# Both products of the MLP by one level of Strassen's algorithm, layer 1 in full before layer 2

## The chip, the cores and the metric

One core of a Trainium2 chip runs the kernel. The metric is the device time of one execution in microseconds. Each time that follows is that of such an execution; a profile is one execution taken by the hardware profiler.

## The reference

2048 tokens of 640 channels go through two sublayers, each with a layer norm, a shift and scale from a condition vector, and a gate. Sublayer A is a causal depthwise convolution along the sequence by way of a Fourier transform; sublayer B is an MLP with squared ReLU. All data are float32.

```
mod = (_silu(c) @ w_mod).reshape(c.shape[0], 6, 1, -1)
sa, ca, ga, sb, cb, gb = ...
h = _layernorm(q, axis=-1) * (1 + ca) + sa
x = q + ga * _A_ref(h, k, v, shift_k, ssm_k, ssm_D)
h = _layernorm(x, axis=-1) * (1 + cb) + sb
h = relu(h @ w1 + b1) ** 2          # w1: 640 x 1728
x = x + gb * (h @ w2 + b2)          # w2: 1728 x 640
```

## The kernel before

The program is recorded as a graph of operations and then ordered by a list scheduler (`Graph.order`, line 227), which runs a model of the five engines and emits each engine's instructions in the order it found. An operation's priority is either a number in the table `URGE` (by group, as ("f1", 0) for layer 1 of chunk 0) or, where the table has none, the longest path from it to the end (`levels`, line 189). After that the order on each engine is fixed, and the engines meet at semaphores. Every recorded operation shows line 444 in the profile, so groups are told apart by their tiles.

**The first part** (to about 277 us of the profile) is sublayer A: for five blocks of 128 channels, transforms by matmuls in plain float32, products of spectra on DVE and POOL, and back. Its result x1 goes to DRAM (`x1_d`), but for the first 512 tokens, which stay in SBUF. Weights of the MLP are loaded and split in its last 50 us.

**The MLP** multiplies by a split: each operand is written as a high part (rounded to fp32r by ACT) and a low part (the rest, by DVE or POOL), and a product is three matmuls: high x high, high x low, low x high. The tokens go in 8 chunks of 256 (`NC`), the inner dimension of 1728 in 14 blocks of 128 (`NF`; the last has 64). For each chunk: `prep_hat` and `prep_xt` (lines 1204, 1213) normalise, transpose, scale and split the tokens into the tile `xt`; for each block f, `mlp_front` (1231) makes layer 1 into one PSUM bank from five k-blocks, `mlp_middle` (1250) adds the bias, squares and splits h into a ring of six small tiles (`hring` and others), and `mlp_back` (1275) multiplies h with w2 into four accumulators of 320 columns; `mlp_out` (1299) multiplies by the gate row, adds x1 and stores. From chunk 1 on, layer 1 takes high x (high, low) in one matmul of 512 columns and low x high in one of 256. All of w1 and w2 stays in SBUF, split (`w_load`, 1146, into tiles `w_S...`, `w_W...`, `w_KA...`). The gate row is made by ten float32 matmuls on a broadcast condition (`w_gate`, lines 1677 to 1697) around the end of the first part, and b2 times the gate is added to x1 by POOL.

The chunks overlap freely: layer 1 of a later block or chunk runs between layer 2 of an earlier one.

Of the kernel before, what the change touches and what calls it, by code (L numbers as in the profile page):

```python
# [29 lines left out]
LAST = 690.0  # L30
# [85 lines left out]
class Buf:  # L116
    __slots__ = ("name", "shape", "dtype", "choices", "real", "cell", "seen", "users", "n", "line", "psum", "left", "end")
# [6 lines left out]
class Graph:  # L124
    def __init__(self):
        self.nodes, self.group, self.bufs = [], None, []
        self.key, self.urge = ("", 0), {}

    def buf(self, name, shape, dtype, choices, cell=32, line=None, psum=False):
# [6 lines left out]
        b.line, b.psum, b.real, b.seen, b.users, b.n = line, psum, None, [], set(), len(self.bufs)  # L136
        self.bufs.append(b)
# [51 lines left out]
    def levels(self):  # L189
# [6 lines left out]
        for b in self.bufs:  # L196
            if len(b.choices) == 1:
                for s in b.choices[0][0]:
                    if s in line:
                        later.setdefault(line[s].n, []).append(b)  # L200
                    line[s] = b
        level = [0.0] * len(nodes)
        blevel = {}
        for n in reversed(nodes):
# [22 lines left out]
    def order(self, lag=0.06, pelag=0.1, phase=0.0):  # L227
# [82 lines left out]
        def early(n):  # L310
            return 1e4 if not n.told else HOLD if n.engine == "SP" and n.key[0] != "out" else 30.0 if n.key[0] == "warm" else 1e4
# [198 lines left out]
def ssm_mlp_kernel(  # L510
# [80 lines left out]
    KV = sb.tile([P, 5120], F32, tag="KV", name="KV")  # L591
    WX = sb.tile([P, 5120], F32, tag="WX", name="wx")
# [17 lines left out]
    work = [part(lambda: WX, 512 * i, (f"W{i}",)) for i in range(10)]  # L610
    work += [part(lambda: WE, 512 * i, (f"W{10 + i}",)) for i in range(2)]
    KACC = [part(lambda: KV, 512 * i, (f"KA{i}",)) for i in range(2)]
    KN = [part(lambda: KV, 1024 + 1024 * i, (f"KN{i}a", f"KN{i}b")) for i in range(4)]
    UT = [part(lambda: KV, 3072 + 512 * i, (f"KN{2 + i // 2}{'ab'[i % 2]}",)) for i in range(4)]
    KVALL = (("KA0", "KA1") + tuple(f"KN{i}{h}" for i in range(4) for h in "ab"), lambda s, d, n: sb.tile(s, d, tag="KV", name=n))
# [12 lines left out]
    def sbuf(name, shape, choices, dtype=F32, line=None):  # L628
        return g.buf(name, list(shape), dtype, choices, line=line)
# [487 lines left out]
    def x1_tile(n):  # L1117
        return sbuf(f"x1_{n}", (P, 2, D), [whole("X1a"), whole("X1b")], line="X1")
# [668 lines left out]
```

## Time and profile before

| | |
|---|---|
| median of 3 runs | 678.6 us (677.04 to 680.27) |
| span of the profiled execution | 678.1 us (the page gives no time around it) |
| TensorE matmul busy | 659.3 us |
| VectorE, ScalarE, GpSimd busy | 408.6, 317.2, 257.2 us |
| first MLP product | 277.29 us |
| HBM read, written | 56.98 MB, 14.42 MB |

PE is TensorE's matmuls, PEld its weight loads, DVE is VectorE, ACT ScalarE, POOL GpSimd, SP the engine that issues most DMAs. A row of a timeline has start, length, engine, operation, "out<-in" by the program's tile names, and a count where like instructions follow each other. A row of a group has, behind the bar, busy time and the mean of one in ns, and then the idle time of its engine before it with what ended it. Matmuls overlap in the pipeline, so the length of one (some 300 ns) is not what it adds to the time; the distance between starts is.

### The profile page before, as it was taken

What the parts mean: (1) busy time and instruction counts of PE and PEld (TensorE: products, weight loads), DVE (VectorE), ACT (ScalarE), POOL (GpSimd) and SP (SyncE); (2) the same over time, 40 slices, a digit from 0 to 9 for tenths busy, and PEclk for the clock granted to TensorE, in tenths of its full rate; (3) what the DMA queues carried; (4) which work ended last, traced back from release to release, by engine and by line L of the source; (5) the groups of instructions that cost most, each with busy time, mean ns of one, the idle gap of its engine ahead of it and who ended that gap; (6) DMA issues with size and microseconds to landing.
All of it is one profiled execution on the core that took longest, in us unless ns stands there. A gap on an engine that the chain in (4) does not pass through costs nothing.

```text
span 678.1 us, 16426 instructions
## 1 busy us (share of the span) xinstructions
PE 659.3 (97%) x6825; PEld 597.1 (88%) x6825; DVE 408.6 (60%) x813; ACT 317.2 (47%) x650; POOL 257.2 (38%) x330
## 2 busy tenths in 40 slices
PE   9989999999899999999999999999999999999996
PEld 8879698789788796899999999999989999999996
DVE  2759677988689767766436562554563562663532
ACT  3654858887655846555225242243232242242220
POOL 2439467779767684362014031021031040040001
PEclk9999999999899999999999999999999999999999
DMA  9799999997785473433020200110110100200011
GB/s 226 222 269 299 265 251 200 260 259 203 186 201 116 90 229 125 126 94 92 1 78 1 78 1 1 22 58 1 23 55 1 44 36 1 69 10 1 4 37 39
DMA packets 108430, 72.45 MB, mean 107 GB/s; under 512 B 48514, under 2 KB 95810, under 8 KB 108356
## 3 DMA queue, kind: packets, MB, share of 16 engines
q1 hardware_dynamic: 106304, 70.80, 40.2%
q8 instruction: 53, 0.87, 0.6%
q10 hardware_dynamic: 1988, 0.61, 0.4%
q14 instruction: 21, 0.17, 0.1%
q0 software_dynamic: 64, 0.01, 0.0%
HBM read 56.98 MB, written 14.42 MB: 105 GB/s over the span
## 4 chain that ended last, share of the span: by engine, by line
PE 83%; DVE 6%; DMA 3%; ACT 3%; issue 2%; POOL 1%; ACTq 0%; SPq 0%; DVEq 0%; POOLq 0%
PE ps L444 83%; DVE KV L444 2%; DMA KV<-in_A_v_dram 1%; DVE mtmp L444 1%; DMA x<-x_d 1%; POOL wx L444 1%; DMA d<-in_A_ssm_D_dram 1%; ACT q L444 1%; DVE s L444 1%; DVE wx L444 1%; DMA out_dram<-x 1%; ACT up L444 1%; POOL wm L444 0%; ACT KV L444 0%; ACT a L444 0%
## 5 line engine op out<-in xcount | busy, mean ns | idle before, releaser
L444 PE MATMUL ps<-xt,w_S 128*128 128x512 f32 (+1 forms) x935 | 174.7, 329 | 0.0
L444 PEld LDWEIGHTS ps<-xt,w_S 128*128 128x128 f32 x935 | 140.9, 188 | 13.5 <-DVE w_S L444 0.2
L444 PE MATMUL ps<-w_S,hring 128*128 128x320 f32 x648 | 110.5, 311 | 0.0
L444 ACT ACTIVATE mtmp<-ps,b1t 128x256 f32<-128x256 f32 (+1 forms) x112 | 50.2, 474 | 112.2 <-PE ps L444 107.2
L444 PEld LDWEIGHTS ps<-w_S,hring 128*128 128x128 f32 x648 | 99.2, 188 | 2.2
L444 DVE TENSOR_TENSOR mtmp<-ps,mtmp 128x256 f32<-128x256 f32 (+1 forms) x99 | 40.5, 419 | 74.2 <-ACT mtmp L444 73.8
L444 PE MATMUL ps<-a,gb 128*64 128x128 f32 x1260 | 76.1, 275 | 3.8 <-DVE wx L444 2.1
L444 PEld LDWEIGHTS ps<-a,gb 128*64 128x64 f32 x1260 | 69.3, 137 | 10.7 <-DVE wx L444 3.3
L444 DVE TENSOR_TENSOR hring<-mtmp,hring 128x256 fp32r<-128x256 f32 x74 | 38.6, 525 | 49.3 <-ACT hring L444 48.8
L444 PEld LDWEIGHTS ps<-cst,p 64*64 64x64 f32 (+1 forms) x1792 | 58.4, 135 | 10.9 <-issue 6.8
L444 PE MATMUL ps<-cst,p 64*64 64x64 f32 (+1 forms) x1792 | 63.9, 244 | 2.4 <-issue 2.2
L444 POOL TENSOR_TENSOR wx<-wx 128x256 f32<-128x256 f32 x80 | 59.8, 766 | 10.6 <-DVE wx L444 8.5
L444 ACT ACTIVATE hring<-mtmp 128x256 fp32r<-128x256 f32 x74 | 30.9, 418 | 69.4 <-PE ps L444 50.5
L444 POOL TENSOR_TENSOR x<-x,gb2row 128x640 f32<-128x640 f32 x16 | 25.6, 1618 | 88.5 <-ACT mtmp L444 73.6
L444 ACT ACTIVATE a<-ps 128x512 f32<-128x512 f32 x72 | 41.3, 616 | 34.2 <-PE ps L444 33.8
L444 POOL TENSOR_TENSOR x<-mtmp,x 128x640 f32<-128x640 f32 (+1 forms) x9 | 13.3, 1483 | 115.5 <-DVE mtmp L444 115.5
L444 PE MATMUL ps<-w_S,w_W 128*128 128x320 f32 x312 | 53.5, 311 | 0.3 <-DVE w_W L444 0.3
L444 PEld LDWEIGHTS ps<-w_S,w_W 128*128 128x128 f32 x312 | 47.7, 188 | 1.4 <-DVE w_W L444 0.6
L444 DVE TENSOR_TENSOR wx<-ps,wx 128x512 f32<-128x512 f32 x64 | 40.7, 681 | 13.0 <-PE ps L444 7.8
L444 DVE SCALAR_TENSOR_TENSOR mtmp<-mtmp 128x256 f32<-128x256 f32 x91 | 43.7, 493 | 1.7
L444 POOL TENSOR_TENSOR mtmp<-mtmp 128x256 f32<-128x256 f32 (+1 forms) x21 | 13.4, 645 | 82.5 <-ACT mtmp L444 82.5
L444 PE MATMUL ps<-gi,wx 64*128 64x128 f32 x640 | 41.8, 284 | 0.0
(142 smaller groups left out, 1092.8 us busy)
## 6 DMA issues: line engine op xcount, KB each, us to landing
wm<-in_w_mod_dram SPq DMA_DIRECT2D x25, 320.0 KB, 4.8
p<-in_A_ssm_k_dram SPq DMA_DIRECT2D x20, 256.0 KB, 4.9
KV<-in_A_k_dram SPq DMA_DIRECT2D x20, 256.0 KB, 4.2
KV<-in_A_v_dram SPq DMA_DIRECT2D x20, 256.0 KB, 5.0
p<-kv_d SPq DMA_DIRECT2D x20, 256.0 KB, 4.6
xp<-in_A_q_dram SPq DMA_DIRECT2D x10, 512.0 KB, 7.8
q<-in_A_q_dram SPq DMA_DIRECT2D x7, 640.0 KB, 5.2
out_dram<-x SPq DMA_DIRECT2D x14, 320.0 KB, 3.8
```

Of the source, the lines that this page charges most:

```text
L444: fn(*real, **{k: a.real() if isinstance(a, View) else a for k, a in kw.items()})
```

## The change

Two matrices cut into 2 x 2 blocks are multiplied with 7 block products in place of 8 (Strassen's scheme in Winograd's form: sums of blocks on both sides, and intermediate sums of products that are used twice). Here this is one level, over the split products as before.

**Layer 1** goes over 4 quarters s of 512 tokens (two chunks a and b) and 6 pairs p of f-blocks. Four of the five k-blocks form the 2 x 2 cut; the fifth is added plainly. A pair takes 18 block products of 128 x 128 x 256 in place of 20. Three PSUM banks x, z, y per pair (two sets in turn) accumulate; x is read by ACT in the middle of its accumulation and then goes on. The last two f-blocks are done plainly (`rest`). The squared result, not split, is stored to a new tensor in DRAM, `h_d`.

**Layer 2** goes over 8 chunks of 256 tokens (two halves i) and the 6 pairs of f-blocks, with seven accumulators of 320 columns (`ps7`), in place of four; block products per pair: 7 for 8. h is read back from DRAM by pairs (two pairs in one tile from chunk 1 on), four sums are made on DVE, and the seven pieces of 128 are split (ACT, DVE) into a ring of four (`ring2`). At the end of a chunk one copy and seven additions join the accumulators. b2 rides as a row in the last w2 block, times a block of ones.

The weights are split with their sums: `w1_pair` on POOL and DVE before and during the first quarter, `w2_pair` in the tiles of w1 as the last quarter frees them. The gate row becomes one sum on POOL and two matmuls, in the first quarter. The large tiles KV and WX are cut in two each.

In the scheduler the numbers of all MLP groups are gone from `URGE`; they are placed by the longest path, with each TensorE operation of the MLP charged its place in the program's order (`turns`), and an early limit for SP and other engines.

```diff
-LAST = 690.0
+LAST = 640.0
+AHEAD = 60.0
+SPARE = 10.0
+LAG = 0.1
...
+            top += LAG
+            if n.engine == "PE" and n.id >= self.mlp:
+                turns = top = max(top, turns)
+                turns += n.cost
...
+    def w1_pair(p):
+        split(w[:, 0, 0:5], w[:, 1, 0:5], r1)
+        split(w[:, 0, 5:8], w[:, 1, 5:8], r2[:, 2:5])
+        for j, (eng, op, l, r) in enumerate((
+            (pool, add, r2[:, 0:2], r2[:, 2:4]),
+            (pool, sub, 0, r1[:, 0:2]),
+            (dve, sub, r1[:, 0:2], r2[:, 0:2]),
+            (pool, sub, r1[:, 2:4], 1),
+            (pool, sub, r1[:, 4:5], r2[:, 4:5]),
+        )):
...
+    def combined(s):
+        halves(2 * s + 1, T2)
+        for j, (l, r) in enumerate(((c[:, 0:2], a[:, 0:2]), (c[:, 2:4], 0), (c[:, 2:4], c[:, 0:2]), (a[:, 2:4], 1))):
+            sub(dve, t, l, made[r] if isinstance(r, int) else r)
+            split(TC[j][:, 0], TC[j][:, 1], t)
...
+    def pair(s, p, before):
+        products(x, [(wb(i), xa(i)) for i in range(2)], True, True)
+        taken(r1[:, 0:CH], x, c1)
+        before()
+        products(z, [(wb(i + 2), xa(i + 2)) for i in range(2)] + [(wb(4), xa(4))], True, True)
+        plus(r1[:, 0:CH], z)
+        products(y, [(wb(8 + i), tc_(0, i)) for i in range(2)] + [(wb(7), xb(4))], True, True)
+        taken(r2[:, CH:], y, c2)
+        products(x, [(wb(10 + i), tc_(1, i)) for i in range(2)], False, True)
+        taken(r1[:, CH:], x, c1)
+        products(y, [(wb(14 + i), xb(i + 2)) for i in range(2)] + [(wb(16), xb(4))], False, True)
+        plus(r1[:, CH:], y)
+        square(r1)
+        h_store(s, f1, r1)
+        products(x, [(wb(12 + i), tc_(2, i)) for i in range(2)], False, True)
+        plus(r2[:, CH:], x)
+        def after():
+            products(x, [(wb(5 + i), tc_(3, i)) for i in range(2)] + [(wb(7), xa(4))], False, True)
+            taken(r2[:, 0:CH], x, c2)
+            square(r2)
+            h_store(s, f2, r2)
...
+    def h_pair(n, p, many=1):
+            sp_dma(t[:, k, 0:4].rearrange("p (j i) t -> p j (i t)", j=2), in_dram(h_d, src, f, f + 2 * P, 1 << n // 2), 1024)
+        add(dve, t[:, :, 4], t[:, :, 0], t[:, :, 2])
+        sub(dve, t[:, :, 5], t[:, :, 4], t[:, :, 1])
+        sub(dve, t[:, :, 6], t[:, :, 1], t[:, :, 0])
+        sub(dve, t[:, :, 7], t[:, :, 3], t[:, :, 5])
+        for k in range(many):
+            h = HS[n, p + k] = ring2[(n * NP + p + k) % 4]
+            split(h[:, 0], h[:, 1], t[:, k, 1:8])
...
+    def l2(acc, h, w, first, last):
+        with g.as_one(0.441):
+            for i, (a, y) in enumerate(((0, 0), (0, 1), (1, 0))):
+                mm(acc, h[a], w[y], first and i == 0, last and i == 2)
+    def second_layer(n):
+        todo = {1: (0, 0), 2: (2, 1), 6: (4, 4), 7: (5, 5), 4: (1, 6), 5: (3, 3), 3: (6, 2)}
+            for i, (a, b) in todo.items():
+                l2(ps7[i], parts(h, a), wv, p == 0, p == NP - 1)
+        copy(act, e1, ps7[1])
+        add(dve, c[:, 1, 0], ps7[2], e1)
+        add(dve, u2, ps7[6], e1)
+        add(dve, u3, ps7[7], u2)
+        add(dve, c[:, 0, 0], ps7[4], u3)
+        add(dve, u2, ps7[5], u2)
+        add(dve, c[:, 0, 1], ps7[5], u3)
+        add(dve, c[:, 1, 1], ps7[3], u2)
```

Where the first part ends, TensorE's order before (`mtmp` are the normalised tokens, `xt` the split ones, `w_S` weights, `wx`/`we` and `cst` the last transforms of the first part):

```order
L444 MATMUL ps_94<-ident,mtmp 128x128
L444 MATMUL ps_93<-ident,mtmp 128x128
L444 MATMUL ps_98<-w_gate 128x320
L444 MATMUL ps_97<-we,cst 64x512
L444 MATMUL ps_97<-wx,cst 64x512
L444 MATMUL ps_98<-w_gate 128x320 x3
L444 MATMUL ps_95<-xt_3701,w_S_2622 128x256 x6
L444 MATMUL ps_97<-xt_3701,w_S_2622 128x256 x3
L444 MATMUL ps_98<-xt_3701,w_S_3407 128x256 x6
```

and after (`up` holds the normalised tokens, `t_0` the split first chunk, `ka` the first two sums of token blocks, `xa` the second chunk, `w_0` and `w_1` the first two weight pairs):

```order
L458 MATMUL ps_99<-we,cst 64x512
L458 MATMUL ps_99<-wxb,cst 64x512
L458 MATMUL ps_93<-ident,up_1718 128x128 x2
L458 MATMUL ps_94<-ident,up_1718 128x128 x2
L458 MATMUL ps_98<-ident,up_1718 128x128 x2
L458 MATMUL ps_95<-t_0_3763,w_0_3025 128x256 x3
L458 MATMUL ps_96<-t_0_3763,w_1_3317 128x256 x3
L458 MATMUL ps_95<-t_0_3763,w_0_3025 128x256 x3
L458 MATMUL ps_94<-t_0_3763,w_0_3025 128x256 x3
L458 MATMUL ps_96<-t_0_3763,w_1_3317 128x256 x3
```

The gate's products are gone from there, the transposes of two chunks stand before the first product in place of one chunk's, and the first products of two pairs alternate.

On DVE at the same place, before (`xfs` are scaled transposes, `xt` their low halves):

```order
L444 TENSOR_TENSOR w_S_3617<-w1s_3587,w_S_3617 128x640
L444 TENSOR_SCALAR xfs<-ps_91,cbs 128x256
L444 TENSOR_TENSOR up_1007<-ps_97,up_1007 128x512
L444 TENSOR_TENSOR xt_3701<-xfs,xt_3701 128x256 x2
L444 TENSOR_TENSOR gb2row<-ps_98,gb2row 128x320
L444 BN_AGGR mv_3636<-s_2495 128x2
L444 TENSOR_SCALAR xfs<-ps_93,cbs 128x256
L444 TENSOR_TENSOR xt_3701<-xfs,xt_3701 128x256
```

and after (`s` holds the last two weight blocks, `we<-xf` are the sums of token blocks):

```order
L458 TENSOR_TENSOR w_4_3715<-up_1718,w_4_3715 128x256
L458 TENSOR_TENSOR s_3643<-w1s_3503,s_3643 128x5x64
L458 TENSOR_SCALAR xf<-ps_93,cbs 128x256
L458 TENSOR_SCALAR xf<-ps_98,cbs 128x256
L458 TENSOR_SCALAR xf<-ps_95,cbs 128x256
L458 TENSOR_TENSOR t_0_3763<-xf,t_0_3763 128x256
L458 TENSOR_TENSOR we<-xf 128x512
L458 TENSOR_TENSOR t_0_3763<-xf,t_0_3763 128x256
L458 TENSOR_SCALAR xf<-ps_97,cbs 128x256
L458 TENSOR_TENSOR t_0_3763<-xf,t_0_3763 128x256
L458 TENSOR_SCALAR xf<-ps_93,cbs 128x256
L458 TENSOR_TENSOR t_0_3763<-xf,t_0_3763 128x256
```

More of the weights' splits are ahead of the first token block, and sums of 512 columns stand between the token blocks' low halves.

In layer 2, around the end of a chunk, DVE's order after the change (`outs` is the joining of the accumulators, `up` the h read back with its sums, `ka`, `kz`, `xa`, `xp1r` the four places of the split ring):

```order
L458 TENSOR_TENSOR up_1718<-up_1718 128x2x128
L458 TENSOR_TENSOR outs<-ps_94,outs 128x320
L458 TENSOR_TENSOR outs<-ps_95,outs 128x320
L458 TENSOR_TENSOR kz<-up_1010,kz 128x896
L458 TENSOR_TENSOR outs<-ps_96,outs 128x320
L458 TENSOR_TENSOR outs<-ps_97,outs 128x320
L458 TENSOR_TENSOR xa<-up_1010,xa 128x896
L458 TENSOR_TENSOR outs<-ps_100,outs 128x320 x2
L458 TENSOR_TENSOR up_1718<-up_1718 128x2x128 x3
L458 TENSOR_TENSOR outs<-ps_99,outs 128x320
L458 TENSOR_TENSOR outs<-outs,gbrow 128x640
L458 TENSOR_TENSOR xp1r<-up_1718,xp1r 128x896
```

Splits of the next chunk's h stand between the additions that free the accumulators; before, DVE's work there was one split of 256 per f-block and four multiplications by the gate per chunk.

More of the change, by code (lines that the diff above doesn't have):

```diff
@@ new lines, in ssm_mlp_kernel, with first_layer @@
+    late = [lambda: None]
+    def first_layer(s):
+        for p in range(NP):
+            late[0] = pair(s, p, late[0])
+            if p == 3 and s + 1 < NS:
+                tokens(s + 1)
+            if s == NS - 1 and p == 4:
+                ring_two()
+                h_pair(0, 0)
+        r = [out_tile(f, s) for f in (NF - 2, NF - 1)]
+        rest(s, 1, r)
+        if s == NS - 1:
+            h_pair(0, 1)
+        late[0]()
+        late[0] = lambda: None
+        if s + 1 < NS:
+            combined(s + 1)
+        rest(s, 0, r)
+        g.key = ("ev", s)
+        square(r[0])
+        square(r[1][:64])
+        h_store(s, NF - 2, r[0])
+        h_store(s, NF - 1, r[1], 64)
```

612 lines of the change are left out of this document (360 added, 252 removed), and 77 rows, old and new, of the table URGE.

## Prediction

> **What bounds the kernel now.** I read the page's head and first part, then the busy time by stage, then who made TensorE wait, then TensorE's timeline where products of one width follow each other.
>
> ```profile
> span 678.1 us, 16426 instructions
> PE 659.3 (97%) x6825; PEld 597.1 (88%) x6825; DVE 408.6 (60%) x813; ACT 317.2 (47%) x650; POOL 257.2 (38%) x330
> ...
> 277.00:323.00 46.00, 45.97 (x347) 45.01 (x346) 28.86 (x47) 25.85 (x55) 19.82 (x22) 1.00 0.37 103
> 358.00:481.00 123.00, 122.66 (x790) 115.17 (x789) 61.97 (x146) 42.82 (x97) 26.18 (x26) 1.00 0.08 22
> 504.67:668.00 163.33, 163.33 (x1049) 154.01 (x1050) 76.01 (x179) 50.18 (x117) 27.66 (x27) 1.00 0.08 21
> ...
> PE ps L444 <- ACT mtmp L444: 0.3, 1, 0.3
> PE ps L444 <- DVE w_W L444: 0.3, 1, 0.3
> ```
>
> In the stage rows the columns are length, then PE, PEld, DVE, ACT and POOL busy, granted clock, DMA share. In 163.33 us of the MLP TensorE has no gap at full clock, DVE is busy 47%, DMA 8%. The only waits of TensorE that fall in the MLP are the last two rows, 0.6 us together. So the MLP lasts as long as its matmuls, and DVE, ACT and the DMAs have room. A change that takes columns from TensorE is paid in full until something else is late.
>
> **TensorE's term.** The price of a product by its width, from starts of neighbouring groups:
>
> ```profile
> 286.32 3.00 PE L444 MATMUL ps<-xt,w_S 128*128 128x256 f32 x24
> 289.16 0.60 PE L444 MATMUL ps<-w_S,w_W 128*128 128x320 f32 x3
> ...
> 435.99 6.48 PE L444 MATMUL ps<-xt,w_S 128*128 128x256 f32 x36
> 442.30 1.92 PE L444 MATMUL ps<-w_S,w_W 128*128 128x320 f32 x12
> ...
> 661.03 3.69 PE L444 MATMUL ps<-w_S,hring 128*128 128x320 f32 x24
> 664.55 0.60 PE L444 MATMUL ps<-w_W 128*128 128x320 f32 x3
> ...
> L444 PE MATMUL ps<-xt,w_S 128*128 128x512 f32 x18 | 6.2, 395 | 0.0
> L444 PE MATMUL ps<-xt,w_S 128*128 128x256 f32 x18 | 4.7, 280 | 0.0
> ```
>
> 24 products of 256 columns took 289.16 - 286.32 = 2.84 us, 0.1183 us each. 24 of 320 took 664.55 - 661.03 = 3.52 us, 0.1467 each. The group at 435.99 is 18 of 512 and 18 of 256 (last two rows); 6.31 us for it leaves 0.232 for one of 512. Before, the code issues in layer 1 455 wide and 730 narrow products (chunk 0: 13 x 15 + 10 narrow; each later chunk 65 wide, 75 narrow) and in layer 2 8 x (13 x 12 + 8) = 1312 of 320: 105.7 + 86.4 + 192.5 = 384.6 us. After, layer 1 has 24 pairs x 18 block products x 3 plus 8 x 25 = 1496 of 256, and layer 2 8 x (6 x 7 x 3 + 20) = 1168 of 320: 177.0 + 171.3 = 348.3 us. **Removed: 36.3 us.** It is not an eighth, as one of five k-blocks in layer 1 and the last two f-blocks stay plain.
>
> The Trainium skill, "TensorE: Matmul & The Clock Gate", section "Back-to-back issue gap", speaks against this term: it gives a sustained 81 ns per matmul at 128 columns and 131 ns at 512, so half the width costs far more than half. Drawn as a line (an estimate from that page) both versions would cost about 270 us and nothing would be removed. By the trace a line through 0.1183 and 0.1467 has under 0.01 us at no columns, so the trace does not agree.
>
> **The start of the MLP.** Before, DVE's last copy of the first part's transform starts at 262.19 and the first product at 277.29:
>
> ```profile
> 262.19 0.68 DVE L444 COPY q<-ps 128x512 f32<-128x512 f32 x1
> ...
> 272.97 1.25 PE L444 MATMUL ps<-ident,mtmp 128*128 128x128 f32 x10
> 274.06 0.70 PE L444 MATMUL ps<-w_gate 128*128 128x320 f32 x2
> ...
> 275.70 1.88 PE L444 MATMUL ps<-w_gate 128*128 128x320 f32 x6
> 277.29 8.32 PE L444 MATMUL ps<-xt,w_S 128*128 128x256 f32 x63
> ...
> L444 PE MATMUL ps<-w_gate 128*128 128x320 f32 x20 | 6.9, 454 | 0.0
> ...
> L444 DVE TENSOR_TENSOR xt<-xfs,xt 128x256 fp32r<-128x256 f32 x5 | 2.0, 423 | 0.3 <-ACT xt L444 0.3
> L444 DVE TENSOR_TENSOR mtmp<-ps,gbrow 128x320 f32<-128x320 f32 x32 | 14.5, 485 | 15.9 <-PE ps L444 15.8
> L444 DVE TENSOR_TENSOR wx<-ps,wx 128x512 f32<-128x512 f32 x64 | 40.7, 681 | 13.0 <-PE ps L444 7.8 <-POOL wx L444 2.7 <-issue 2.5
> L444 DVE TENSOR_TENSOR x<-mtmp,x 128x640 f32<-128x640 f32 x7 | 5.8, 824 | 0.2
> L444 DVE SCALAR_TENSOR_TENSOR mtmp<-mtmp 128x256 f32<-128x256 f32 x91 | 43.7, 493 | 1.7
> ```
>
> The gate's 20 matmul records go (6 in 1.59 us at 275.70, so 5.3 us), and 4 come back later. I count nothing for them: TensorE would only wait longer, since DVE feeds the first product. DVE's price is 0.42 us for 256 columns, 0.48 for 320, 0.68 for 512, 0.82 for 640, by that slope 1.09 for 896; with three operands 0.49 for 256, so 0.76 for 512; in a row each starts 0.07 earlier than that. (Ten transposes, 272.97 to 274.06, are 0.11 each.) From the copy to the low half of the first token block DVE had 28 instructions before (13.0 us); after, 43 (17.9 us: four pairs' weight splits and combinations are finished first). That is 4.8 us more on an engine that idled about 2 us there. Against it TensorE and ACT do less there. I take the first product at 281.3, **4.0 later** (bounds 0, if DVE's idle time and other engines absorb it; 8, if the weight work queued ahead also delays the first part). Then 14 more DVE instructions (the second chunk and the four sums) pace the next 21 block products, 7.4 us on TensorE: 0.8 more (0 to 2).
>
> **The first quarter of layer 1.** TensorE needs 374 x 0.1183 = 44.2 plus 20 transposes and the gate, 47.5 us. DVE's order holds 105 instructions there (37 of 512, 14 of them with three operands, 23.9 us; 48 of 256, 16.7; the rest 6.0), 46.6 us by the prices above. POOL's eight weight differences (5.5 us) and the gate's four sums (6.3) stand beside it. A POOL operation and a DVE operation on SBUF hold each other up:
>
> ```profile
> L444 POOL TENSOR_TENSOR wx<-wx 128x256 f32<-128x256 f32 x80 | 59.8, 766 | 10.6 <-DVE wx L444 8.5 <-DMA xp<-in_A_q_dram 1.4
> L444 POOL TENSOR_TENSOR wm<-wm,wm 128x640 f32<-128x640 f32 x20 | 31.4, 1572 | 15.1 <-ACT wm L444 14.8
> ...
> L444 ACT ACTIVATE mtmp<-ps,b1t 128x256 f32<-128x256 f32 x104 | 46.4, 474 | 105.5 <-PE ps L444 100.6 <-DVE hring L444 3.6 <-DVE w_W L444 1.1
> ...
> 286.06 3.45 POOL L444 TENSOR_TENSOR x<-x,gb2row 128x640 f32<-128x640 f32 x2
> ...
> 286.59 1.51 DVE L444 TENSOR_TENSOR hring<-mtmp,hring 128x256 fp32r<-128x256 f32 x1 [0.20 <-ACT hring L444]
> ```
>
> The DVE operation took 1.51 us instead of 0.42. By these rows POOL pays 0.77 us for 256 columns and 1.57 for 640, ACT 0.47 for an accumulator. If a third of POOL's 12 us falls on DVE, DVE needs 51; TensorE has two pairs of PSUM banks as slack: **2.5 us** (0 to 8). The other quarters have 31 to 33 us of DVE work for 46: 0.5 each, 1.5 (0 to 4). There the new waits (an accumulator may go on only when ACT has read it) have 9 block products or 3.2 us of cover against ACT's 0.47; behind a waiting product every other accumulator's products queue, so a late ACT would show at once. The 56 stores of h (256 KB, some one per 3 us) meet a DMA that is 8% busy; SP's queue holds them in DVE's order, ahead of weights needed 10 us later.
>
> **Between the layers.** Layer 2's weights reuse layer 1's tiles, and h comes back from DRAM. From the last product of layer 1 to the first that needs pair 5 stand some 19 to 21 us of TensorE work; DVE has 23 us listed by then and just after (splits of h, two weight pairs), POOL eight subtractions of about 0.85. I take **3 us** (0 to 8).
>
> **Layer 2.** A chunk of 256 tokens is 146 x 0.1467 = 21.4 us. DVE has per chunk 12 sums of 256 (0.35), 6 splits of 896 (1.02), the last block 1.4, seven additions from PSUM (0.41) and four of 640 (0.75): 17.6 us, 82%, without POOL beside it. All seven accumulators end within 3 us and eight banks exist, so a late DVE operation stops TensorE at the next chunk's first pair. Cover there is 2.6 us per bank, against up to 1.1 us of a split ahead of it. I take 0.5 per chunk, **4 us** (0 to 16). The reads of h must also arrive:
>
> ```profile
> p<-kv_d SPq DMA_DIRECT2D x20, 256.0 KB, 4.6
> ...
> x_d<-xp SPq DMA_DIRECT2D x15, 256.0 KB, 3.4
> x<-x_d SPq DMA_DIRECT2D x6, 640.0 KB, 4.1
> ```
>
> A double pair is 2 x 256 KB, so between 4.1 and 9.2 us. A buffer serves three doubles (load X, then 3.5 us on DVE) and one last block (about 6.4) in two chunks, 42.8 us: 3X + 16.9 fits up to X = 8.6. I take X = 6, hidden; at 9.2 it is 0.9 us a chunk. SP's queue puts a chunk's stores and the residual's load ahead of the next reads; I leave that to the range.
>
> **The end.** After the last product, before:
>
> ```profile
> 671.30 1.19 PE L444 MATMUL ps<-w_KA,hring 128*128 128x320 f32 x7
> 672.53 0.49 DVE L444 TENSOR_TENSOR mtmp<-ps,gbrow 128x320 f32<-128x320 f32 x1 [0.24 <-PE ps L444]
> 672.94 0.89 DVE L444 TENSOR_TENSOR x<-mtmp,x 128x320 f32<-128x320 f32 x2
> ```
>
> TensorE ends at 672.5, DVE at 673.8, the span 4.3 later. After, DVE still owes about two PSUM additions, four multiplications and four additions of 320 (0.41 each), 4.3 us, then the same 4.3: **3.2 us more** (2 to 4.5). Transposes (80 before and after) cancel; the moved gate (five loads of 320 KB on SP between weight loads and x1's stores, five ACT scalings, four POOL additions, two products) is needed only at chunk 0's output, some 190 us later, and hurts only by POOL's share above.
>
> **The sum.** Before, 277.3 + 384.6 + 7.7 of transposes would end at 669.6; it ended at 672.5, so 2.9 us were small losses that my terms replace. 678.1 - 36.3 - 2.9 + 4.0 + 0.8 + 2.5 + 1.5 + 3 + 4 + 3.2 = 657.9; with 10 transposes counted inside the old start, 1.1 less, and the gate back, 1.1 more, it stays. I round to 658. The page gives no time around the span; the median of the runs, 678.6, is 0.5 above it, within their spread of 3.2, so 658 stands for both.
>
> **Rivals.**
> - *TensorE bounds throughout.* The start costs 0 to 1, DVE's lateness is absorbed, only the end is longer: 678.1 - 36.3 - 2.9 + 1 + 3.2 + 1 = 644. For it: DVE is under 85% nearly everywhere and the before stages show no gap. Against: the first quarter's 46.6 of 47.5. Chance 0.22 (640 to 650).
> - *DVE becomes the bound of the first quarter and of layer 2.* All of POOL's 12 us fall on DVE (+8), and each chunk loses 1.5 us: 658 + 5.5 + 8 = 671. Chance 0.15 (665 to 676).
> - *The reads of h pace layer 2, and it is slower.* Place: the two h buffers. 20 us of forecast gain are 2.5 a chunk, 5 in two: 3X + 16.9 = 47.8, X = 10.3. At X = 12, 53 us per two chunks, about 41 more: 699. The longest row is 2 x 4.6; the reads wait behind other transfers on one queue. Chance 0.05. The same side would be reached if a product cost by number and not by columns: the 36.3 go and 694 is left, which the rates above exclude to a hundredth, 0.01.
> - That it doesn't do what it says is excluded: TensorE's order holds exactly 1496 and 1168 products.
>
> **Chances.** Forecast 0.57 (650 to 665), the others as above. The range leaves out about 0.1 at each end: 643 to 673. About 0.5% (3.4 us) is what a measurement of this kernel can tell from no change; faster by more than that 0.92, within it 0.03, slower 0.05.
>
> **What would show it.** Right: 256-wide products still at 0.118 us and 320-wide at 0.147; the first product near 281; DVE near 90% busy for the 48 us after it and waits of TensorE there; layer 2 at 21.5 to 22.5 us a chunk with DVE about 82% busy; 8.5 us from the last product to the end. Wrong: DVE idle while TensorE waits in layer 2 (then the reads of h), a price per product that grew, or a first part that ends later.

## The result, and the profile after

| | before | after |
|---|---|---|
| median | 679.4 us (677.04 to 680.27, 4 runs) | 689.39 us (689.02 to 689.64, 4 runs) |
| span of the profiled execution | 678.1 us | 687.2 us |
| first MLP product | 277.29 us | 301.12 us |

After to before is 1.0155, 95% interval [1.0134, 1.0177]: slower by 1.6%. Forecast were 658 us and a gain of 3%. The profiled execution of the changed kernel took 689.02 us, 1.8 more than its span.

The head of the page of the changed kernel, with the clock's row (40 slices of 17.2 us, tenths of full speed):

```profile
span 687.2 us, 17238 instructions
PE 637.4 (93%) x6976; PEld 589.4 (86%) x6976; DVE 521.9 (76%) x981; ACT 359.1 (52%) x685; POOL 223.7 (33%) x294
PEclk9999999999999999569999999999998999999998
```

TensorE is busy 21.9 us less, and yet the span is 9.1 longer: idle time came in. The dip of the clock, slices 17 and 18, lies where the MLP begins. The busy time by stage of the changed kernel (length; PE, PEld, DVE, ACT, POOL busy with counts; clock; DMA share; GB/s):

```profile
175.00:220.00 45.00, 41.11 (x780) 34.82 (x778) 33.37 (x55) 23.83 (x49) 29.28 (x39) 0.98 0.77 172
220.00:240.00 20.00, 16.39 (x531) 14.41 (x530) 12.67 (x23) 15.81 (x35) 12.81 (x12) 0.91 0.28 55
240.00:271.00 31.00, 29.14 (x497) 24.79 (x488) 26.29 (x41) 17.39 (x37) 24.55 (x32) 1.00 0.24 65
271.00:301.00 30.00, 19.58 (x67) 9.92 (x68) 21.56 (x45) 12.37 (x29) 8.92 (x10) 0.58 0.53 167
301.12:357.25 56.13, 51.50 (x402) 50.21 (x401) 44.25 (x97) 36.57 (x76) 10.32 (x9) 0.95 0.34 108
357.25:497.25 140.00, 139.24 (x1164) 137.86 (x1164) 101.25 (x204) 74.88 (x153) 18.38 (x18) 1.00 0.38 126
497.25:530.00 32.75, 27.51 (x157) 25.15 (x156) 29.00 (x54) 14.74 (x24) 7.23 (x7) 0.90 0.40 120
530.00:676.00 146.00, 146.00 (x997) 146.00 (x997) 120.32 (x222) 46.05 (x66) 0.00 (x0) 1.00 0.44 138
```

and the same view of the kernel before, where the first part ends:

```profile
175.00:220.00 45.00, 43.65 (x874) 37.96 (x872) 37.19 (x62) 27.12 (x55) 30.04 (x40) 0.97 0.72 164
220.00:240.00 20.00, 19.88 (x555) 14.79 (x555) 14.85 (x21) 16.59 (x35) 11.65 (x11) 1.00 0.44 98
240.00:261.00 21.00, 21.00 (x367) 20.05 (x364) 14.82 (x21) 12.26 (x22) 19.01 (x27) 1.00 0.66 203
```

TensorE's busy time is 2.5 us less by 220 and 3.5 less from 220 to 240, in a part whose arithmetic the change doesn't touch; then it is idle for a third of the last 30 us before the MLP. The second to fourth quarter and layer 2 after 530 are full. TensorE's timeline of the changed kernel has the marks between the stages:

```profile
268.18 2.50 PE L458 MATMUL ps<-gi,wxb 64*128 64x128 f32 x32 [0.77 <-ACT q L458]
...
301.12 4.61 PE L458 MATMUL ps<-t,w 128*128 128x256 f32 x27
...
320.75 1.65 PE L458 MATMUL ps<-xa,w 128*128 128x256 f32 x6 [3.91 <-ACT up L458]
...
354.13 3.12 PE L458 MATMUL ps<-t,s 128*128 128x256 f32 x25
...
494.13 3.12 PE L458 MATMUL ps<-t,s 128*128 128x256 f32 x25
497.09 1.92 PE L458 MATMUL ps<-w,xp1r 128*128 128x320 f32 x12
...
677.71 1.04 PE L458 MATMUL ps<-w,xa 128*128 128x320 f32 x6
```

The last groups of 25 end a quarter each (25 x 0.1183 = 3.0 us). In the table each piece stands against the forecast's (137.1 is 1122 products at 0.1183 and 40 transposes at 0.11):

| piece | forecast | measured | over |
|---|---|---|---|
| up to the first MLP product | 281.3 | 301.12 | +19.8 |
| first quarter with its pacing | 47.5 + 0.8 + 2.5 = 50.8 | 354.13 + 3.0 - 301.12 = 56.0 | +5.2 |
| other three quarters | 137.1 + 1.5 = 138.6 | 497.09 - 357.1 = 140.0 | +1.4 |
| change of layers and layer 2 | 171.3 + 3 + 4 = 178.3 | 677.71 + 6 x 0.1467 - 497.09 = 181.5 | +3.2 |
| end | 8.5 | 687.2 - 678.6 = 8.6 | +0.1 |

The forecasts of the pieces add to 657.5, 0.4 us under the sum as it was stated; with the 29.7 over they make 687.2. Two thirds of the miss lie before the first product. The kernel before ended its last inverse transform of that kind at 260.9, of which this row of its timeline has the start:

```profile
255.29 5.63 PE L444 MATMUL ps<-gi,wx 64*128 64x128 f32 x96
```

After, the same group ends at 268.18 + 2.50 = 270.7. So 9.8 us are lost before that mark, and the stretch from it to the first product went from 16.4 to 30.4 us, 14.0 more. The chain that ended last, of the changed kernel, names what the first part of that stretch waits for (start, length, what):

```profile
269.69 0.88 POOL up L458
...
270.63 0.53 POOL up L458
...
271.18 3.40 DMA w1s<-in_B_w_dram
...
274.60 0.74 ACT w L458
...
275.37 0.26 DVE w L458
275.63 0.48 issue
276.11 0.95 DVE up L458
277.06 0.61 DVE we L458
277.68 0.04 issue
277.72 2.00 PE ps L458 x4
```

Read it backwards. TensorE's transforms at 277.72, the first of the first part's last four such groups, wait for DVE's copy `we`, a step of the first part. That copy stands in DVE's queue behind a weight's low half (`w`) and a sum of weights (`up`). The low half waits for ACT's high half, that one for a weight load, and the load for its staging buffer `w1s`, which POOL had held until its last sum of weights was made. The low half is the fourth of six of 640 columns on DVE, one for each weight pair, so it belongs to the fourth pair. In TensorE's order that pair's first product is the 115th of the MLP, and it starts here:

```profile
315.97 0.87 PE L458 MATMUL ps<-t,w 128*128 128x256 f32 x6
```

So the first part waits for weights that TensorE reads 38 us later. Later in the chain the same shows once more: the last group of transforms, at 297.30, waits for a copy that stands behind 2.1 us of weights' low halves on DVE (from 294.51). DVE is 72% busy in the stretch (21.56 of 30 us); no engine is full.

### The profile page after: what moved, and what is told of

It is laid out like the page before. It is cut to its first block, busy times and chain, and to the rows that moved or that the text cites. A ratio compares the mean times of both kernels' runs of the same rounds, so it can differ in the third digit from the quotient of the medians.

```text
span 687.2 us, 17238 instructions
## 1 busy us (share of the span) xinstructions
PE 637.4 (93%) x6976; PEld 589.4 (86%) x6976; DVE 521.9 (76%) x981; ACT 359.1 (52%) x685; POOL 223.7 (33%) x294
## 4 chain that ended last, share of the span: by engine, by line
PE 75%; DVE 11%; issue 4%; ACT 4%; DMA 3%; POOL 2%; DVEq 0%; SPq 0%; ACTq 0%; POOLq 0%
PE ps L458 75%; DVE up L458 2%; DVE kva L458 1%; ACT up L458 1%; DVE w L458 1%; DVE wxb L458 1%; DMA kvb<-in_A_k_dram 1%; POOL wxb L458 1%; DVE s L458 1%; DMA d<-in_A_ssm_D_dram 1%; DVE wxa L458 1%; DVE outs L458 1%; ACT a L458 1%; DMA w2s<-in_B_w_dram 1%; DVE kvb L458 1%
## 5 line engine op out<-in xcount | busy, mean ns | idle before, releaser
L458 ACT ACTIVATE up<-ps,b1t 128x256 f32<-128x256 f32 (+1 forms) x112 | 52.3, 472 | 57.8 <-PE ps L458 53.3
L458 PE MATMUL ps<-t,w 128*128 128x256 f32 x432 | 63.8, 286 | 0.0
L458 PEld LDWEIGHTS ps<-t,w 128*128 128x128 f32 x432 | 56.6, 192 | 0.2 <-DVE t L458 0.2
L458 ACT ACTIVATE a<-ps 128x512 f32<-128x512 f32 x72 | 40.6, 612 | 30.4 <-PE ps L458 29.9
L458 DVE TENSOR_TENSOR up<-up 128x256 f32<-128x256 f32 (+1 forms) x124 | 44.3, 397 | 13.5 <-DMA up<-h_d 12.7
L458 DVE SCALAR_TENSOR_TENSOR up<-up 128x512 f32<-128x512 f32 (+1 forms) x56 | 39.6, 712 | 9.7 <-ACT up L458 9.3
L458 POOL TENSOR_TENSOR wm<-wm,wm 128x640 f32<-128x640 f32 x24 | 38.0, 1582 | 23.9 <-ACT wm L458 23.6
L458 PE MATMUL ps<-kz,w 128*128 128x256 f32 x288 | 43.8, 288 | 0.8 <-ACT up L458 0.6
L458 PE MATMUL ps<-ka,w 128*128 128x256 f32 x288 | 42.2, 281 | 0.0
L458 PEld LDWEIGHTS ps<-kz,w 128*128 128x128 f32 x288 | 37.8, 191 | 1.6 <-ACT up L458 0.8
L458 PE MATMUL ps<-w,kz 128*128 128x320 f32 x216 | 38.2, 315 | 0.0
```

What stands on the lines that cost most here:

```text
L458: fn(*real, **{k: a.real() if isinstance(a, View) else a for k, a in kw.items()})
```

## The experiments

Each changes one thing, in the changed kernel unless said otherwise. "Ratio" is to the kernel before, run on the same chip.

**Is the order to blame?** The orders ahead of the prediction show where first part and MLP meet; the numbers of `URGE` for the first part are the same in both kernels. The longest path gives the MLP's groups due times from 236 on (weight splits) and 238 (first product), and the first part's last groups carry 259 to 291, so they stand behind (a smaller number goes first). This run gives the MLP groups later or earlier due times; every instruction is the same.

```diff
-LAST = 640.0
-AHEAD = 60.0
-SPARE = 10.0
+LAST = 623.0
+AHEAD = 52.0
+SPARE = 255.0
...
-                n.prio -= LAST
+                n.prio -= LAST + self.later.get(n.key, 0.0)
...
+    g.later = {
+        ("b1", 0): 72.3, ("ev", 0): -73.6, ("ev", 3): 14.1, ("hat", 2): -72.8, ("hat", 3): -127.5,
...
+        ("xc", 0): -194.9, ("xs", 0): -141.9, ("xs", 1): -352.4, ("xs", 2): -140.8, ("xs", 3): -154.2,
```

> The changed kernel with the same instructions; only the due times of the MLP's work are moved (the three constants of the placing rule and an offset for each of 41 groups), so that the order on each engine's queue is another. Theory PLACE (the time went where the MLP's preparation stands in the queues of ScalarE, VectorE and SyncE between 175 and 357 us and again around 497 us): of the 19 us by which the first product comes later than forecast, the 9 us by which the first quarter is longer than the others (56.1 against 47) and the 10 us at the change of layers, half to two thirds come back: 664 to 672, first MLP product at 286 to 292. Rival CLOCK (TensorE works at half clock there since the gate's ten products are gone) and rival AMOUNT (there is simply more vector work before the first quarter is done): neither is changed by an order, 682 to 690.

673.74 us (672.22 to 675.51), ratio 0.9926 [0.9897, 0.9955]. The time falls by 15.7 us, 1.7 short of the range that the order theory gave, and 8 from the rivals'. First product and stage row:

```profile
289.48 1.90 PE L458 MATMUL ps<-t,w 128*128 128x256 f32 x13 [0.56 <-ACT xf L458]
```

```profile
220.00:240.00 20.00, 18.97 (x540) 14.47 (x533) 11.98 (x22) 17.19 (x37) 11.98 (x11) 1.00 0.49 119
```

2.6 of the 3.5 us that were lost between 220 and 240 are back: most of that loss was the order's.

**Is the clock to blame?** 84 idle products of 128 columns were put at 14 places around the start of the MLP.

```diff
+            if n.engine == "PE" and (n.key in (("t", 4), ("y", 4)) or n.key in (("xt", 0), ("xt", 1)) and n.nth == 0):
+                self.fill(n, n.calls[0][2][0].real())
...
+                nc.tensor.transpose(o, ident, ident)
```

> The changed kernel in its own order, with six idle products (128x128, of the identity) put ahead of each of the 14 groups of TensorE's work that wait between 268 and 300 us; each writes the PSUM region that the group itself writes next. CLOCK: the granted clock of 263 to 320 us goes from 0.74 and 0.78 to near 1, the 42 us that TensorE is busy there shrink by a quarter, and the time falls by 8 to 11 us, to 678 to 681. PLACE and AMOUNT: TensorE waits for what comes late from ScalarE and VectorE, at any clock; the time stays within 4 us of 689.4 (685 to 693) even where the clock rises.

691.06 us (690.06 to 692.28), ratio 1.0181 [1.0155, 1.0207]; first product 300.98. The two stages around it, of the changed kernel and then with the idle products:

```profile
263.00:290.00 27.00, 19.20 (x157) 13.37 (x152) 19.37 (x40) 13.70 (x30) 11.02 (x13) 0.74 0.31 99
290.00:320.00 30.00, 23.12 (x142) 18.20 (x142) 26.87 (x59) 17.13 (x37) 5.46 (x7) 0.78 0.29 90
```

```profile
263.00:290.00 27.00, 21.57 (x201) 17.61 (x196) 18.78 (x39) 13.62 (x30) 10.33 (x12) 1.00 0.32 99
290.00:320.00 30.00, 22.79 (x170) 19.41 (x168) 26.01 (x58) 16.34 (x36) 4.87 (x6) 1.00 0.29 91
```

The granted clock rises from 0.74 and 0.78 to 1.00 and the first product moves by 0.14 us. The low clock is a mark of the idle time, not what makes it. (The Trainium skill, "TensorE: Matmul & The Clock Gate", section "What's actually happening", says that the clock is throttled by default and activity releases it; the rows agree, and show that releasing it gains nothing while TensorE waits for others.)

**Did the gate's ten products cover the start before?** In the kernel before they were made to follow its first MLP product.

```diff
+    after = [x for x in g.nodes if x.key == ("f1", 0) and x.engine == "PE"][0]
+    for x in g.nodes:
+        if x.key == ("gate", 0) and x.engine == "PE":
+            x.deps.add(after.id)
```

> The kernel before, with the gate's ten f32 products held back until the first product of layer 1 has been issued, so that TensorE has nothing to fill its waits between 260 and 277 us with, as in the changed kernel. CLOCK: the granted clock falls below 0.85 between 260 and 280 us and the first MLP product comes at 283 us or later instead of 277.3; 690 or more. PLACE and AMOUNT: the first MLP product stays at 277 (within 2 us), and the kernel gets longer only by the ten products themselves, which now stand between MLP products (some 5.4 us of TensorE): 683 to 688.

685.73 us (683.35 to 687.04), ratio 1.0099 [1.0062, 1.0136], but the first product comes at 276.87, no later than the 277.29 of before, and the clock stays full:

```profile
260.00:280.00 20.00, 16.22 (x120) 10.67 (x118) 18.25 (x35) 11.35 (x22) 5.33 (x5) 1.00 0.52 141
```

So it is not their removal that sets the start; the forecast had counted nothing for it either. The 7 us are lost later. By the expectation 5.4 of them are the products themselves, which no longer stand in TensorE's waits; that was not followed.

**Only the weights later.** The splits, sums and loads of pairs 1 to 5 due 60 us later.

```diff
-                n.prio -= LAST
+                n.prio -= LAST + (60.0 if n.key[0] in ("w1s", "w1c") and n.key[1] or n.key[0] == "lw1" and n.key[1] > 1 else 0.0)
```

> The changed kernel with the due time of one thing moved: the splitting and summing of layer 1's weights of pairs 1 to 5 (and their loads) counts as due 60 us later, behind the first part's last work. If it is only the queue ahead of the first part's last work that costs (PLACE in its simple form), the first product comes 8 to 15 us earlier than 301.1, layer 1 ends as much earlier than 497.3, and the time falls to 675 to 681. If ScalarE and VectorE have a sum of work to do before the first quarter can end (AMOUNT), the first product comes earlier, but the first quarter, 56.1 us, grows by more than that: layer 1 ends at 505 or later, and the time is 695 to 710. CLOCK says nothing of an order: 689 within 3.

699.26 us (one run). The first product comes at 283.12, 18 us earlier, and the first quarter then takes until 369.4:

```profile
283.00:369.40 86.40, 63.20 (x425) 56.23 (x425) 64.28 (x130) 48.44 (x104) 22.40 (x22) 0.90 0.38 118
```

TensorE is busy 63 of 86 us. The simple form of the order theory (675 to 681) is refuted, and the range given for too much work (695 to 710) is met, as far as one run can say. The start that was forecast is to be had, but work pushed out of the way as one block comes due in the quarter behind it.

**Are the sums of the weights to blame?** The order of every engine stays as it is; the 150 instructions that sum weights (48 on ACT, 54 on DVE, 48 on POOL) are left out, so that the products read plain blocks of the same weights in their place (layer 2 has the same edits).

```diff
+        start = len(g.nodes)
...
+        for n in g.nodes[start:]:
+            n.calls = []
...
-        wb = lambda k: parts(w, k) if k < 16 else (e[:, 0], e[:, 1])
+        wb = lambda k: other(parts(w, k) if k < 16 else (e[:, 0], e[:, 1]), parts(w, k % 8))
```

> The changed kernel with the order of every engine kept, and without the instructions that make and split the sums and differences of the weights in both layers (48 on ScalarE, 54 on VectorE, 48 on GpSimd; the products that would use a sum read a plain block of the same weights, so TensorE does the same work on other numbers). AMOUNT (ScalarE and VectorE have too much to do between 263 and 357 us, and the sums are what Strassen adds to it): the four pairs split before 301 us lose about 8 us of ScalarE's and 9 of VectorE's work, so the first product comes at 291 to 295 instead of 301.1, the first quarter takes 48 to 52 instead of 56.1, layer 2 with the change of layers 175 to 178 instead of 181.7: 666 to 676 in all. PLACE in its pure form (late loads and instructions that stand ahead of the first part's last ones decide, and the sums fill waits): first product at 297 or later, 681 to 688.

671.38 us (671.22 to 672.48), ratio 0.9879 [0.9855, 0.9904]. First product:

```profile
290.64 2.59 PE L458 MATMUL ps<-t,w 128*128 128x256 f32 x13
```

10.5 us earlier, while the mark before it (end of the last inverse transform of that kind, 271.05) stays: what the sums cost at the start lies wholly in the second stretch, 19.6 us here against 30.4. SP's waits there, first of the changed kernel from 258 to 274, then of this one from 250 to 271, show the link of the chain that went:

```profile
SPq L669 <- POOL up L458: 12.4, 2, 11.2
```

```profile
SPq L669 <- DVE w L458: 15.4, 3, 10.9
```

The change of layers and layer 2 took 177.3 us here against 181.5, as expected. The first quarter took 55, not the 48 to 52 expected: the sums are not what makes it long.

**With the sums of the token blocks left out as well** (their instructions are emptied in the same way):

```diff
-        tc_ = lambda j, i: parts(TC[j], i)
+        tc_ = lambda j, i: other(parts(TC[j], i), parts(T1[s], i))
```

> As the kernel without the sums of the weights (order of every engine kept), and also without the four differences of x that each quarter makes and splits (per quarter 8 instructions of VectorE, 5.4 us, and 4 of ScalarE, 2.5 us; the products that would use a difference read a plain block of x). What bounds the first quarter is open: two instructions moved in VectorE's queue changed nothing (689.2), the wait only took another name. AMOUNT: VectorE, 90% busy from 290 to 320 us, is the bound of the first quarter, so it falls from 55.1 to 49 to 51 and the time from 671.4 to 665 to 668; the other quarters, where VectorE is 65% to 75% busy, stay at 47. If the first quarter is bound by what stands in the queues and not by their sum, 54 to 56 and 669 to 672.

671.73 us (670.07 to 674.41), ratio 0.9897 [0.9863, 0.9932]: nothing more is gained. The quarter takes 55.1 us, and TensorE's wait is there still:

```profile
309.70 2.02 PE L458 MATMUL ps<-xa,w 128*128 128x256 f32 x9 [3.57 <-ACT up L458]
```

**The wait in the first quarter.** Two DVE instructions of the first part's end (the last `up<-ps,up` and `xp<-xp,up`) were moved ahead of the next statistics; then the same without the sums of weights; then, beside the first move, the second quarter's statistics and normalising about 15 us later on DVE and ACT.

```diff
-    g.emit(g.order())
+    order = g.order()
+    late = [o for o in order if o[2].key in (("yc", 4), ("fin", 4)) and o[2].engine in ("DVE", "POOL")]
...
+    order[i + 1 : i + 1] = move
+    ahead = [o for o in order if o[2].key in (("st2", 2), ("st2", 3), ("hat", 2), ("hat", 3)) and o[0] > 290]
...
+    order[i:i] = ahead
+    g.emit(order)
```

> The changed kernel with two instructions moved on VectorE and nothing else: the first part's last product (up<-ps,up at 317.36) and its last add (xp<-xp,up at 319.50), whose input TensorE has ready at 299.3, stand right behind the split of the first x (near 304.4) instead of behind the statistics of the next quarter's x. PLACE: ScalarE's eviction at 320.22 no longer waits for the piece of memory that the add frees, the wait of 3.9 us that TensorE has at 316.8 goes, and with it the slow clock of the 5 us after it (0.66, some 1.7 us): 683 to 686, layer 1 ends at 491 to 494 instead of 497.3. If another thing ends just after it (the statistics, a weight that is late), 1 to 2 us at most come back: 687 to 689. CLOCK and pure AMOUNT say nothing of an order: 689 within 2.

> The kernel without the sums of the weights (order kept) and with the two instructions moved: both of the edits that were tried alone. If the wait of 3.57 us that is left at 306 us in the kernel without sums has the same cause as the one at 316.8 in the changed kernel, 4 to 6 us come off the 671.4: 665 to 668, the first quarter takes 49 to 52 instead of 55.1. If the first quarter is long for another reason, 670 to 672.

> The changed kernel with the two instructions of VectorE moved as before, and also the statistics and the normalising of the second quarter's x (16 small instructions of VectorE, 6 of ScalarE; 8 us of work on the two) moved about 15 us back in both queues, behind the first quarter's squares and evictions of these 15 us; they are needed only at 340. PLACE for the first quarter: the wait of 2.8 to 3.9 us that TensorE has near 317 us for an eviction, with the slow clock after it, is ScalarE and VectorE doing the next quarter's x first; it goes, the first quarter takes 50 to 53 instead of 56.1, and the time falls to 683 to 686. If the evictions wait for the memory that the stores of h have to free first, the wait stays near 3 us: 688 to 690.

689.17 us (688.35 to 690.82, ratio 1.0161 [1.0143, 1.0178]), 671.21 (670.0 to 676.04, 0.991 [0.9883, 0.9937]) and 690.04 (688.02 to 692.32, 1.0172 [1.0139, 1.0205]): none gained anything against its counterpart. TensorE's longest wait in the quarter, in the first and then the third:

```profile
321.55 1.65 PE L458 MATMUL ps<-xa,w 128*128 128x256 f32 x6 [2.78 <-ACT up L458]
```

```profile
326.06 1.65 PE L458 MATMUL ps<-kz,w 128*128 128x256 f32 x6 [4.02 <-DVE up L458]
```

The wait stays (3.9 us in the changed kernel) and changes its name. ScalarE's rows of the changed kernel show what the eviction (`up<-ps,b1t`) stood behind there:

```profile
317.48 1.73 ACT L458 ACTIVATE x<-x,nm,rs 128x640 f32<-128x640 f32 x2 [0.43 <-DVE nm L458]
320.22 0.47 ACT L458 ACTIVATE up<-ps,b1t 128x256 f32<-128x256 f32 x1 [1.00 <-DVE xp L458]
```

It is the normalising of the second quarter's tokens, which waits for DVE, and then DVE again: a chain of two queues, not one instruction. The third run bears this out, though it gained nothing. There statistics and normalising stand at 320.7 to 327.4, and the eviction that TensorE waits for, now one of DVE's, stands right behind them; its products follow at 326.06:

```profile
325.58 0.42 DVE L458 TENSOR_TENSOR up<-ps,up 128x256 f32<-128x256 f32 x1
```

So the wait went where the block went. The other theory of that run, that evictions wait for memory which the stores of h must free, gave 688 to 690 us, near what was measured, but the rows don't show it: ScalarE's evictions waited for a store once between 301 and 330, for 0.4 us in the changed kernel and 0.9 in the third run.

**One place in the first part.** TensorE stood 3.6 us for ACT's copies `a<-ps`, which ACT did after eleven normalisings (`up<-xp,nm,rs`). The two copies were moved ahead of them. ACT's rows of the changed kernel, and the group that waited:

```profile
222.47 4.32 ACT L458 ACTIVATE up<-xp,nm,rs 128x128 f32<-128x128 f32 x11
226.69 1.09 ACT L458 ACTIVATE a<-ps 128x512 f32<-128x512 f32 x2
```

```profile
227.93 3.59 PE L458 MATMUL ps<-gi,wxb 64*128 64x128 f32 x32 [3.61 <-ACT a L458]
```

```diff
+    c = [o for o in order if o[2].key == ("pac", 4) and o[2].nth in (6, 7) and o[2].engine == "ACT"]
...
+    order = [o for o in order if o not in c]
+    i = min(i for i, o in enumerate(order) if o[2].key == ("pra", 4) and o[2].engine == "ACT" and o[0] > 217)
+    order[i:i] = c
```

> The changed kernel, in which ScalarE's two copies a<-ps that end TensorE's 3.6 us wait before 227.93 stand ten instructions earlier in its queue, ahead of the normalising (up<-xp,nm,rs) that it did from 222.5 to 226.8; nothing else is moved and the same work is done. QUEUE (the first part is late because single instructions stand behind other work in an engine's queue, and each such place is paid in full): the wait before that group falls from 3.6 to under 0.5 us, the first part's last group ends 3 to 4 us earlier (267 to 268 in place of 270.7), the first MLP product comes at 297 to 298.5, and the time is 685 to 686.5. ELSEWHERE (the queue is late as a whole, and the wait takes another name a few us on, as it did in the first quarter when two VectorE instructions were moved): the first MLP product stays within 1 us of 301.1 and the time within 688.4 to 690.

686.29 us (685.19 to 687.36), ratio 1.0117 [1.0096, 1.0138]: 3.1 us less than the changed kernel, as the queue theory had it, and the first product at 299.00, half a microsecond past its range, in a profiled execution that took 687.36 us. The last group of the first mark ends at 269.8 (expected 267 to 268); in this profile the group ahead of the place already starts 1.6 us later than in the other, with nothing changed before it. The group that waited:

```profile
225.77 2.03 PE L458 MATMUL ps<-gi,wxb 64*128 64x128 f32 x32
```

It has no wait any more. Here a place in a queue is paid almost in full; in the first quarter it was not.

**All due times once more.** The numbers were chosen again, per instruction, with transfers counted 15% and 1.2 us longer in the scheduler's model. They cover the first part's own instructions after 165 us too (`comb`, `h`, `fin`), which the earlier choice had left alone.

```diff
+            n.prio -= self.single.get((*n.key, i), 0.0)
...
-                        dma_free = start + n.dma
-                        land = dma_free + 1.0
+                        dma_free = start + (1.15 if t > 165 else 1.0) * n.dma
+                        land = dma_free + (2.2 if t > 165 else 1.0)
```

> The changed kernel with the same instructions and again another order, from due times of all single instructions after 165 us, chosen with transfers counted 15% and 1.2 us longer than before. The sums cost 18 us with the order kept (671.4 without them), and a first choice of due times took 15.7 off (673.7); both brought the first product to 290. If a better order can hide most of the sums, 662 to 669, first product at 286 to 291, first quarter 49 to 53, change of layers (to the end of TensorE's work) 176 to 179; if the first choice had found what an order can give, 671 to 676.

669.59 us (667.2 to 672.79, 6 runs), ratio 0.9876 [0.9845, 0.9906], first product 288.94: the whole change is 1.2% faster than the kernel before, with not one instruction other than in the version that is 1.6% slower. Whether the kernel before would gain from a new choice as well was not tried.

```profile
290.00:320.00 30.00, 29.53 (x230) 28.89 (x231) 28.16 (x61) 16.89 (x40) 6.76 (x7) 0.95 0.46 152
```

The 30 us behind its first products are nearly full (29.53), without the wait of 3.9 us that the changed kernel has 20 us after its first product. Over the whole first quarter less is gained: its 402 matmuls take 53.4 us from 288.94 on, of which TensorE is idle 1.8, against 56.0 and 4.6 for 401 in the changed kernel.

**Order and sums at once:** the order of the last kernel, and the sums of weights left out as above.

> Both at once: every engine's order as in the kernel whose due times were chosen again (669.6 us, first MLP product at 288.9), with the 150 instructions that sum the weights of both layers left out (so the block products read plain blocks, and the products are wrong by that). It asks what is left of the loss once order and sums are both taken away. ONE COVER (order and sums cost the same wait, the sums cost nothing once they stand in a good place): first product 287.5 to 289, time 667 to 670. TWO COSTS (order and sums each cost something of their own; before started its products at 277.3): first product 277 to 284, time 656 to 665, that is, near the forecast of 658.

663.02 us (661.35 to 664.39), ratio 0.9778 [0.9758, 0.9798]. TensorE's first products:

```profile
283.85 0.36 PE L459 MATMUL ps<-t,w 128*128 128x256 f32 x1
284.99 2.28 PE L459 MATMUL ps<-t,w 128*128 128x256 f32 x17 [0.79 <-DVE t L459]
288.67 0.38 PE L459 MATMUL ps<-ka,w 128*128 128x256 f32 x1 [1.40 <-ACT up L459]
```

Two costs, then, that share a part. By the ratios, in per cent of before: order alone takes away 2.8 (2.3 by the MLP's due times alone), sums alone 2.8, both 3.8. In the bad order the sums cost 19 us, in a good one 0.98%, 6.7 us (by the two intervals some 4 to 9). Between 663 and the forecast 5 us are left, which were not followed.

## Why the prediction was wrong

**The step that failed** is the start of the MLP, "4.0 later", bounds 0 and 8. It was 23.8 later. The step counted what DVE does between two marks (43 instructions, 17.9 us) and let the first part end where it ended before. Both halves fell.
- *The first part ended 9.8 us later.* The forecast named "if the weight work queued ahead also delays the first part" within its bound of 8, but looked only at the last 15 us, where first product and transforms meet. The orders part long before that: the first weight load is issued at 174.00 us in place of 183.95, and TensorE's own order differs from 183 us on, for all MLP work had lost the numbers that kept it behind the first part. The due times alone bring 15.7 and 19.8 us (two runs), one pair of copies 3.1.
- *The stretch to the first product took 14.0 us more*, where 4 was forecast. DVE's count was right; its busy time was the wrong price. From its copy `q` at 271.73 to the first low half of a token block at 300.69, DVE took 29.0 us for the same 43 instructions. Weight load, high half, low half and sums pass between SP, ACT, DVE and POOL, and the order in each queue is fixed, so one instruction that waits holds the first part's steps behind it: DVE stood idle 2.95 us before the low half at 275.37. Leaving out the sums took 10.5 us from it.

With both causes gone the first product comes at 283.85, 6.6 us later than before: inside the bounds, and what remains of the step as it was meant.

**Columns: right.** 997 products of 320 columns in 146.00 us are 0.1464 each, against 0.1467. The rule of the Trainium skill ("TensorE: Matmul & The Clock Gate", section "Back-to-back issue gap"), by which the narrower products would have saved nothing (an estimate from its two figures), is refuted here once more.

**First quarter: mechanism in part, size too small.** 3.3 was forecast over TensorE's own 47.5, 8.5 came. It was to be DVE, slowed by POOL; but POOL was busy 10.3 of 56 us and DVE 44, and without any sums the wait stayed. TensorE was idle 4.6 us, most of it in the one wait for an eviction that stands behind the next quarter's normalising, and only new orders of the whole removed that wait. Which instructions of them suffice stays open. The rest of the 8.5 are products that stood further apart, at a granted clock of 0.95.

**Other quarters: size.** 1.5 forecast (0 to 4), 2.9 measured; its cause was not followed.

**Change of layers and layer 2: size, and moved.** 3 and 4 were forecast, 10.2 measured, nearly all of it before 530; 4.2 of it go with the sums of weights. TensorE is idle 5.2 us from 497 to 530, longest before this group, and its products stand further apart there, at a clock of 0.90:

```profile
522.80 1.43 PE L458 MATMUL ps<-s,xp1r 128*128 128x320 f32 x3 [2.17 <-ACT s L458]
```

It waits for ScalarE's high half of a weight block; what holds that up was not followed. Layer 2 behind 530 lost nothing, DVE 82% busy there as forecast.

**End: right**, 8.6 for 8.5. Against the 5.6 of before that is 3.0 more; the sum carried 3.2.

**The rivals.** TensorE bounding throughout and DVE bounding layer 2 both fell. The rival on the other side had h's reads pace layer 2: 146.00 of 146.00 us busy after 530 excludes it. The result went to its side by another mechanism; "a first part that ends later" stood in the forecast as a sign of its being wrong, but with no price and no chance. It should have been that rival: numbers that ordered the work were being deleted, and the order views showed what came ahead.

The columns were saved, then: 36.3 us, and the 2.9 of small losses. Against them came 23.8 before the first product, 8.5 in the first quarter, 2.9 in the others, 10.2 at the change of layers and 3.0 at the end, 48.4 together.

## What to carry to other kernels

When a change takes out numbers that order a program, ask first which instructions of the untouched part now stand behind new work on every queue, and price that over the whole stretch in which the orders differ, not only where the new work begins. An engine that is 72% busy can still be late: follow one buffer through its load, its users and its release across the queues before counting added work as hidden. And test an arithmetic saving and an instruction order apart from each other: here the same instructions ran in 689 and in 670 us.

## What was not expected of the hardware

Granting TensorE its full clock over 57 us (0.74 and 0.78 to 1.00) moved the first product by 0.14 us and gained nothing in time (691.1 against 689.4 us), since TensorE's groups waited there for other engines.
